# A linear-attention and gated feed-forward block on one core: the second layernorm's sums taken from accumulated outputs, the query exponentials in two pieces, and another order of work

## The chip, the cores and the metric

The kernel runs on one core of a Trainium2 chip. A core has TensorE for matmuls (PE in the profile), VectorE (DVE), ScalarE (ACT), GpSimd (POOL) and SyncE (SP), which here issues DMAs. All of them run their own list of instructions in order and wait for each other by semaphores. SBUF is the working memory, PSUM holds matmul results in eight banks, and HBM the inputs and the output. The metric is the device time of one execution in microseconds; the time before is the median of three runs.

## What is computed

Two residual blocks on `x` of 2048 x 640 in bf16. With `LN(x) = (x - mean) / sqrt(var + 1e-5)`:

```python
qkv = LN(x) @ wqkv                       # 32 heads of 20
pq, pk = q @ w_phi, k @ w_phi            # per head
phi_q = concat([softmax(pq), softmax(-pq)])
phi_k = concat([softmax(pk), softmax(-pk)])
kv, z = phi_k.T @ v, sum(phi_k)          # over the 2048 rows
o = (phi_q @ kv) / (phi_q @ z + 1e-6)
h = x + o @ wo
n = LN(h)
out = h + ((n @ w_gate) * (n @ w_up)) @ w_down   # 640 -> 1536 -> 640
```

## The kernel before

The 2048 rows are 16 tiles of 128 rows (partitions); the 640 columns are five chunks of 128 for the contractions. Names carry the tile's number: `h3` is the residual step of tile 3.

*Prologue.* TensorE runs ten matmuls on zeros (`warm`). The key weights arrive in five row chunks (`wk0` to `wk4`), are transposed on TensorE (`WT`, L392), copied out of PSUM (`WTe`) and folded with `w_phi` (`w5`, masked by `Ph`) into a key-feature weight (`F1`, L411, copied out by `Fe1`). The first tiles of `x` are normalised (`L1s`, `L1a` on VectorE, L428 to L431; `L1l` and `L1e`, a Ln and an Exp, on ScalarE; `L1n` on POOL; `xn`) and transposed on TensorE (`xt`, `xte`). Later tiles are transposed by DMA from SP (`xt4` to `xt15`). The query weights come in by transposing DMAs (`wqt`) and are folded later (`F0`).

*Keys and values.* For each tile, projections `V` and `K` (L482, ten matmuls each), `Ve` copies V out, `Kx` makes the two exponentials, `Ks` sums them (VectorE), `Kr` and `Ke` turn the sums into factors (ScalarE), `Kn` scales (POOL, L518), and `KV` (L526) accumulates over all tiles in two PSUM banks. `KVe` copies the result.

*Queries.* `Q` (L482) fills a pair of PSUM banks; `Qx` makes exponentials with both signs out of it (L553 twice and L554 once for each sign, as a pair's second bank also holds the last 40 columns); `Qs` sums (L557), `Qr`, `Qb`, `Qe`, `Qn` scale one half; `qT` transposes by DMA; `N` (L589) multiplies with the key-value matrix; `dd`, `rd`, `o` (L600, L603, L606) divide; `oT` transposes by DMA (L610); `O` (L616) is the output projection.

*Second layernorm.* `h` (L620) adds the projection to `x` in place. `L2s` takes the statistics of its two halves (L626, L627), `L2a` joins them to mean and variance (L629). `hc` (L638 on VectorE or L639 on ScalarE) writes the centred rows, negated, `hT` transposes them by DMA (L643). The scaling is left until the end, as gate and up are both linear in it: `L2v` adds epsilon on POOL (L630) and `L2r` takes the reciprocal (L632), which `y` applies.

*Feed-forward.* Five blocks of rows (tiles 0 to 1, 2 to 5, 6 to 9, 10 to 13, 14 to 15). Each has 12 pairs of a gate and an up matmul group (`U`, L658, named block, column, 0 or 1); `g` copies the gate out (ScalarE, L663), `u` multiplies it with the up half (VectorE, L666). `D` (L677) is the down projection of a tile, `y` (L689) scales by `L2r`'s result and adds `h`, `w` writes to HBM.

*What sets the order.* The table `PLAN` in the text gives each named operation a place in time, a choice of engine where it has alternatives (`alts`), and its slots (PSUM banks, buffers). `arrange` sorts each engine's operations by that place, and `emit` puts in the semaphore waits that data and slots call for. So the order is written out by hand, engine by engine, and a slot is free once the last user of its previous holder is done. Loads are issued by SP and by ScalarE's queue.

The lines that follow are those that the change touches.

Of the kernel before, what the change touches and what calls it, by code (L numbers as in the profile page):

```python
# [48 lines left out]
x0:0.7:1 w5:1.18:1 wk0:1.18 wv0:4.06 wk1:2.14 wv1:2.62 wk2:1.66:1 wv2:3.58:1 wk3:2.62:1 wv3:4.06 wk4:3.1 wv4:4.54:1 x1:0.7 x2:2.14:1 x3:1.66 x4:3.58:1  # L49
x6:3.1 x8:5.02:1 x10:5.02 x12:4.54:1 x14:21.015 wqt0:13.874 wqt1:9.289 wqt2:26.055 wqt3:6.94 wqt4:19.655 wo0:27.415 wo2:34.715 wd0:35.195 wd1:47.175  # L50
wd2:49.392 wd3:37.595 wg0:32.875 wu0:5.5 wg1:37.115 wu1:6.46 wg2:40.335 wu2:25.575 wg3:36.635 wu3:5.98 wg4:35.675 wu4:36.155 id0:0.9 gl0:1.2 eps:0.7
id1:1.45 gla0:2.07 glb0:2.51 gla4:2.29 glb4:4.51 gla1:2.73 glb1:3.17 gla2:3.39 glb2:4.73 gla3:1.85 glb3:2.95 va1:6.664 phz:3.61 ekz:6.364 rqz:6.064
Sz:7.734 mk0:6.164 mk1:7.484 mk2:7.934 zero:0.7 warm0:1.08 warm1:1.51 warm2:1.94 warm3:2.37 warm4:2.8 warm5:3.23 warm6:3.66 warm7:4.09 warm8:4.52::0
warm9:4.74 Ph0:4.95 Ph1:5.609 Ph2:5.743:1 WT0:4.96::1 WTe0:5.509 WT1:6.769::5 WTe1:7.329:1 WT2:5.836::0 WTe2:6.386 WT3:7.725::2 WTe3:8.85 WT4:8.886::0
WTe4:9.922 F1_0:6.342::6 Fe1_0:8.676:1 F1_1:8.162::4 Fe1_1:9.299 F1_2:7.219::0 Fe1_2:8.052:1 F1_3:9.509::6 Fe1_3:10.766 F1_4:10.953::0 Fe1_4:11.538:1
L1s0:3.993 L1a0:5.633 L1s1:4.813 L1a1:6.1 L1s2:7.03 L1a2:9.686 L1s3:6.21 L1a3:10.215 L1s4:11.145 L1a4:12.785 L1s5:11.965 L1a5:13.005 L1s6:13.115
L1a6:14.353 L1s7:10.325 L1a7:12.895 L1s8:20.053 L1a8:21.803 L1s9:20.983 L1a9:23.833 L1s10:14.463 L1a10:20.873 L1s11:15.283 L1a11:19.443 L1s12:28.423
L1a12:34.233 L1s13:25.363 L1a13:30.243 L1s14:26.183 L1a14:34.123 L1s15:31.773 L1a15:34.013 L1l0:6.132 L1e0:7.229 L1l1:7.009 L1e1:7.952 L1l2:10.546
L1e2:11.389 L1n2:11.899 L1n3:11.699 L1l4:14.835 L1e4:15.678 L1n4:16.588 L1n5:16.188 L1n6:16.388 L1n7:15.988 L1l8:24.376 L1e8:24.806 L1n8:28.209
L1n9:28.409 L1n10:25.45 L1n11:25.65 L1l12:34.675 L1e12:35.518 L1n12:35.895 L1n13:36.095 L1n14:38.854 L1n15:36.295 xn0:7.85::0 xt0:8.53::3 xte0:9.268:1  # L60
xn1:8.35::1 xt1:9.165::1 xte1:9.796:1 xn2:12.875:1:3 xt2:17.252::7 xte2:17.978 xn3:12.161:1:2 xt3:13.17::0 xte3:13.935:1 xn4:19.553::2 xt4:21.495
xn5:17.025:1:0 xt5:18.295 xn6:18.943::1 xt6:22.855 xn7:23.333::3 xt7:24.215 xn8:29.243::1 xt8:30.155 xn9:29.743::3 xt9:31.515 xn10:26.408:1:0
xt10:27.895 xn11:27.745:1:2 xt11:33.355 xn12:36.631:1:0 xt12:45.815 xn13:36.758::1 xt13:38.075 xn14:39.692::2 xt14:47.712 xn15:38.118:1:3 xt15:40.815
V0_0:14.536::0 V0_1:14.807 V0_2:15.079 V0_3:15.351 V0_4:15.622 Ve0:20.238::2 K0_0:9.866::2 K0_1:10.138 K0_2:10.681 K0_3:12.083 K0_4:12.898
# [8 lines left out]
Ks8:41.966::1 Kr8:43.566 Ke8:44.634 Kn8:45.961 KV8:48.538 V9:44.463::4 Ve9:46.092::0 K9:36.997::6 Kx9_0:38.831::2 Kx9_1:39.665 Ks9:40.498::0
Kr9:42.379 Ke9:43.242 Kn9:43.602 KV9:51.842 V10:49.125::6 Ve10:51.708:1:3 K10:46.093::2 Kx10_0:48.562::3 Kx10_1:49.455 Ks10:50.288::3 Kr10:51.925
Ke10:52.788 Kn10:53.419 KV10:56.233 V11:54.874::2 Ve11:57.303:1:1 K11:40.029::4 Kx11_0:41.756::4 Kx11_1:42.619 Ks11:43.452::2 Kr11:45.647 Ke11:49.305
Kn11:50.82 KV11:59.265 V12:63.655::2 Ve12:65.321:1:4 K12:56.548::4 Kx12_0:58.176::0 Kx12_1:59.01 Ks12:59.843::1 Kr12:61.48 Ke12:62.583 Kn12:63.355
# [841 lines left out]
```

## Time and profile before

| | |
|---|---|
| median of 3 runs | 274.31 us (273.6 to 274.59) |
| profiled execution, its span | 272.2 us |
| TensorE busy, instructions | 266.0 us, 2103 |
| VectorE | 171.0 us, 315 |
| ScalarE | 116.6 us, 307 |
| POOL | 73.9 us, 107 |
| `h` (L620) | 16 of 813 ns |
| L626, L627 (statistics of h) | 16 of 481, 16 of 476 ns |
| L629 (aggregate) | 16 of 196 ns |
| L639, L638 (`hc`) | 13 of 828, 3 of 514 ns |
| L553, L554 (`Qx`) | 64 of 442, 32 of 239 ns |
| L518 (`Kn`), L571 (`Qn`), L564 (`Qb`) | 16 each of 2357, 1307, 240 ns |

The profiled execution is one run; its span goes from the first to the last instruction and is 2.1 us under the median. Busy times are unions over an engine's instructions. TensorE's matmuls are pipelined and their ends are modelled, so a stretch shown as fully busy can hold small waits; differences of starts show them.

### The profile page before, as it was taken

How to read it: one execution, taken by the hardware profiler on the slowest of the kernel's cores; microseconds unless marked ns; L12 is line 12 of the kernel's file. 1: busy time of each engine (PE TensorE's matmuls, PEld its weight loads, DVE VectorE, ACT ScalarE, POOL GpSimd, SP SyncE). 2: the span in 40 equal slices, each digit the busy share in tenths (PEclk: the TensorE clock that was granted, in tenths of full speed). 3: DMA queues.
4: the chain of work that ended last, by engine and by line, in shares of the span. 5: the costliest groups of instructions: out<-in, count | busy, mean ns of one | idle time of the engine just before them, and what ended most of it. 6: DMA issues, size and time to landing. Idle time of an engine off the chain costs nothing.

```text
span 272.2 us, 5234 instructions
## 1 busy us (share of the span) xinstructions
PE 266.0 (98%) x2103; PEld 177.2 (65%) x2103; DVE 171.0 (63%) x315; ACT 116.6 (43%) x307; POOL 73.9 (27%) x107
## 2 busy tenths in 40 slices
PE   7899999999989999999999999999999999999996
...
GB/s 201 375 265 162 176 264 313 234 157 108 107 78 160 147 185 110 165 130 98 0 48 48 2 1 43 100 95 43 31 0 2 0 0 51 48 0 0 26 48 55
...
## 3 DMA queue, kind: packets, MB, share of 16 engines
...
q14 instruction: 8, 0.07, 0.1%
HBM read 11.00 MB, written 2.62 MB: 50 GB/s over the span
## 4 chain that ended last, share of the span: by engine, by line
PE 93%; ACT 3%; DMA 2%; ACTq 1%; issue 0%; DVE 0%; DVEq 0%
PE ps L658 38%; PE ps L482 23%; PE ps L677 19%; PE ps L616 8%; DMA ev<-in_A_wqkv_dram 2%; PE ps L526 2%; ACT ph L553 2%; PE ps L589 1%; PE ps L411 1%; ACTq L285 1%; PE ps L462 0%; ACT ph L554 0%; PE ps L392 0%; ACT L884 0%; DVE Wp L689 0%
## 5 line engine op out<-in xcount | busy, mean ns | idle before, releaser
L658 PE MATMUL ps<-xnT,Wgu 128*128 128x512 bf16 (+1 forms) x600 | 105.2, 336 | 0.0
L658 PEld LDWEIGHTS ps<-xnT,Wgu 128*128 128x128 bf16 x600 | 58.5, 98 | 44.2 <-DVE ev L666 0.4
L663 ACT ACTIVATE gt<-ps 128x512 bf16<-128x512 f32 (+1 forms) x60 | 30.5, 511 | 91.4 <-PE ps L658 74.0
L482 PE MATMUL ps<-Wp,xnT 128*128 128x320 bf16 (+1 forms) x480 | 68.6, 299 | 0.8 <-ACT ph L554 0.8
L666 DVE TENSOR_TENSOR ev<-ps,gt 128x512 bf16<-128x512 f32 (+1 forms) x60 | 32.8, 577 | 47.4 <-PE ps L658 34.0
L482 PEld LDWEIGHTS ps<-Wp,xnT 128*128 128x128 bf16 x480 | 45.6, 97 | 18.4 <-ACT ph L554 0.9
L677 PE MATMUL ps<-Wd,ev 128*128 128x320 bf16 (+2 forms) x396 | 53.7, 295 | 0.0
L677 PEld LDWEIGHTS ps<-Wd,ev 128*128 128x128 bf16 x396 | 38.0, 98 | 14.5
L518 POOL TENSOR_TENSOR ek<-ek,SR 128x1280 bf16<-128x1280 bf16 x16 | 37.6, 2357 | 6.7 <-ACT SR L503 6.6
L689 DVE SCALAR_TENSOR_TENSOR Wp<-ps,rs,x_all 128x640 bf16<-128x640 f32 (+3 forms) x18 | 14.5, 808 | 32.9 <-PE ps L677 32.7
L553 ACT ACTIVATE ph<-ps 128x300 bf16<-128x300 f32 x64 | 23.8, 442 | 7.9 <-PE ps L482 7.4
L630 POOL TENSOR_SCALAR ln<-mv 128x1 f32<-128x1 f32 x16 | 3.3, 210 | 84.6 <-DVE mv L629 73.4
L557 DVE TENSOR_REDUCE S<-ph 128x66 f32<-128x1320 bf16 x16 | 24.2, 1515 | 3.1 <-ACT ph L554 3.1
L498 DVE TENSOR_REDUCE SR<-ek 128x64 f32<-128x1280 bf16 x16 | 23.4, 1472 | 1.3 <-ACT ek L494 1.2
L616 PE MATMUL ps<-Wo,Wp 128*128 128x320 bf16 x160 | 23.9, 299 | 0.3 <-ACT RQ L567 0.3
L494 ACT ACTIVATE ek<-ps 128x640 bf16<-128x640 f32 x32 | 22.3, 714 | 2.7 <-PE ps L482 2.4
L571 POOL TENSOR_TENSOR ph<-ph,RQ 128x660 bf16<-128x660 bf16 x16 | 20.9, 1307 | 6.2 <-ACT RQ L567 6.2
L639 ACT ACTIVATE xn<-x_all,mv 128x640 bf16<-128x640 bf16 x13 | 10.7, 828 | 24.2 <-DVE mv L629 24.2
L616 PEld LDWEIGHTS ps<-Wo,Wp 128*128 128x128 bf16 x160 | 15.2, 98 | 6.6 <-issue 0.6
L620 DVE TENSOR_TENSOR x_all<-ps,x_all 128x640 bf16<-128x640 f32 x16 | 13.0, 813 | 4.5 <-PE ps L616 4.4
L606 DVE TENSOR_TENSOR o<-ps,sm 128x720 bf16<-128x720 f32 x16 | 14.2, 894 | 0.1
L428 DVE BATCH_NORM_STATS2 st<-x_all 128x6 f32<-128x320 bf16 x16 | 7.6, 472 | 3.3 <-DMA x_all<-in_A_x_dram 3.3
...
## 6 DMA issues: line engine op xcount, KB each, us to landing
...
```

The source lines that it names most:

```text
L482: ins = e.matmul(pb(b, hb)[:, 0:n1 - n0], lhsT=T["xnT"][:, NC - 1 - c, P * t:P * (t + 1)], rhs=T["Wp"][:, POS[kind], c, n0:n1], start=(c = ...
L494: G.op("act", "%sx%d_%d" % (nm, t, s), lambda e, s=s, b=b, ek=ek: e.activation(out=T["ek"][:, ek.slots[0], 0:2 * D].rearrange("p (b h s f) ...
L498: G.op("dve", "%ss%d" % (nm, t), lambda e, ek=ek, sr=sr: e.tensor_reduce(out=T["SR"][:, sr.slots[0], 0, :], in_=T["ek"][:, ek.slots[0], 0: ...
L518: G.op("pool", "Kn%d" % t, lambda e, ek=ek, sr=sr: e.tensor_tensor(out=T["ek"][:, ek.slots[0], 0:2 * D].rearrange("p (h f) -> p h f", f=DH ...
L553: e.activation(out=o_, in_=i_.rearrange("p (g j f) -> p g j f", j=3, f=DH), func=AF.Exp, scale=1.0 - 2.0 * sg)
L557: G.op("dve", "Qs%d" % t, lambda e, t=t, ph=ph: e.tensor_reduce(out=T["S"][:, t, 0:66].rearrange("p (g k) -> p g k", k=6), in_=pv(ph).rear ...
L571: return e.tensor_tensor(out=v, in0=v, in1=T["RQ"][:, rq.slots[0], 1, 0:33].rearrange("p (g j) -> p g j", j=3).unsqueeze(3).to_broadcast([ ...
L616: ins = e.matmul(pb(b, hb)[:, 0:320], lhsT=T["oT"][:, oT.slots[0], c, :], rhs=T["Wo"][:, c, 320 * hb:320 * (hb + 1)], start=(c == 0), stop ...
L658: ins = e.matmul(pb(b)[:, 0:n], lhsT=T["Wgu"][:, gu, c, P * ft:P * (ft + 1)], rhs=T["xnT"][:, NC - 1 - c, o0:o0 + n], start=(c == 0), stop ...
L663: G.op("act", "g%d_%d" % (bi, ft), lambda e, pg=pg, gt=gt, n=n: e.activation(out=T["gt"][:, gt.slots[0], 0:n], in_=pb(pg)[:, 0:n], func=AF ...
L666: o_ = G.op("dve", "u%d_%d" % (bi, ft), lambda e, pu=pu, gt=gt, hh=hh, ft=ft, n=n: e.tensor_tensor(out=T["hh"][:, hh.slots[0], ft, 0:n], i ...
L677: ins = e.matmul(pb(b, hb)[:, 0:w], lhsT=T["hh"][:, hh.slots[0], ft, P * tt:P * (tt + 1)], rhs=T["Wd"][:, ft, c0 + w * hb:c0 + w * (hb + 1 ...
```

## The change

1. `h` becomes a scalar-tensor-tensor operation (projection times 1.0 plus x) that also writes the row sums. `L2s` and `L2a` fall away. `hc` now computes `sum - 640 h` from that sum, on either engine. A new ScalarE operation `L2q` takes the Square of the same expression and accumulates it over the row; its 640 values per row go to `junk`, ten buffers that lie over `ek`, so that it waits for the last `KV`. `L2v` divides by 640 and adds the epsilon, scaled by 640 squared, and the reciprocal makes up for the factor.
2. `Qx` has two instructions for each sign instead of three: one over 2 x 300 columns of both banks, and the 40.
3. `L1n`, `Kn`, `Qb`, `Qn` and `L2v` may now run on VectorE.
4. All of `PLAN` is replaced: places, engines and slots.

```diff
+H_C = 0.84
...
-                G.op("pool", "L1n%d" % t, lambda e, t=t: e.tensor_scalar(
+                G.op("pool", "L1n%d" % t, lambda e, eng, t=t: e.tensor_scalar(
                     out=T["nb"][:, t:t + 1], in0=T["mv"][:, t, 0:1], scalar1=T["rs"][:, t:t + 1], scalar2=-1.0, op0=ALU.mult,
-                    op1=ALU.mult), 0.2, LP, [rs_b[t], mv_b[t]], [nb_b[t]], 10 * t - 25)
+                    op1=ALU.mult), 0.2, LP, [rs_b[t], mv_b[t]], [nb_b[t]], 10 * t - 25, alts=[("dve", 0.07, LD)])
     KVB = [Buf("kvps%d" % k, "psum") for k in range(2)]
     for t in range(NT):
...
-        G.op("pool", "Kn%d" % t, lambda e, ek=ek, sr=sr: e.tensor_tensor(
+        G.op("pool", "Kn%d" % t, lambda e, eng, ek=ek, sr=sr: e.tensor_tensor(
             out=T["ek"][:, ek.slots[0], 0:2 * D].rearrange("p (h f) -> p h f", f=DH),
             in0=T["ek"][:, ek.slots[0], 0:2 * D].rearrange("p (h f) -> p h f", f=DH),
             in1=T["SR"][:, sr.slots[0], 1, :].unsqueeze(2).to_broadcast([P, 2 * H, DH]), op=ALU.mult),
-            pool_c(1280), LP, [ek, sr], [ek], kk)
+            pool_c(1280), LP, [ek, sr], [ek], kk, alts=[("dve", dve_c(1280), LD)])
         def kv(e, t=t, ek=ek, va=va):
...
-                i0, i1 = pb(b, 0)[:, 0:300], pb(b, 1)[:, 0:300]
-                for o_, i_ in ((v[:, 0:5], i0), (v[:, 5:10], i1)):
-                    e.activation(out=o_, in_=i_.rearrange("p (g j f) -> p g j f", j=3, f=DH), func=AF.Exp, scale=1.0 - 2.0 * sg)
+                e.activation(out=v[:, 0:10].rearrange("p (b g) j f -> p b g j f", b=2),
+                             in_=pp(b, 0, 300).rearrange("p b (g j f) -> p b g j f", j=3, f=DH), func=AF.Exp, scale=1.0 - 2.0 * sg)
...
-            G.op("act", "Qx%d_%d" % (t, sg), qx, 2 * act_c(300) + act_c(40), LA, [b], [ph], kk)
+            G.op("act", "Qx%d_%d" % (t, sg), qx, act_c(600) + act_c(40), LA, [b], [ph], kk)
...
-        def qb(e, rq=rq):
+        def qb(e, eng, rq=rq):
...
-        G.op("pool", "Qb%d" % t, qb, 0.24, LP, [rq], [rq], kk)
+        G.op("pool", "Qb%d" % t, qb, 0.24, LP, [rq], [rq], kk, alts=[("dve", 0.1, LD)])
...
-        G.op("pool", "Qn%d" % t, qn, pool_c(660), LP, [ph, rq], [ph], kk)
+        G.op("pool", "Qn%d" % t, qn, pool_c(660), LP, [ph, rq], [ph], kk, alts=[("dve", dve_c(660), LD)])
...
-        G.op("dve", "h%d" % t, lambda e, t=t, b=b: e.tensor_tensor(
-            out=T["x"][:, t, :].rearrange("p (b n) -> p b n", b=2), in0=pp(b, 0, 320),
-            in1=T["x"][:, t, :].rearrange("p (b n) -> p b n", b=2), op=ALU.add), dve_c(640, True), LD, [b, x_b[t]], [x_b[t]], kk - 2)
-        s2, m2, v2, r2 = Buf("s2%d" % t), Buf("m2%d" % t), Buf("v2%d" % t), Buf("r2%d" % t)
+        sh, sq, v2, r2 = Buf("sh%d" % t), Buf("sq%d" % t), Buf("v2%d" % t), Buf("r2%d" % t)
         rs2_b.append(r2)
-        def l2(e, t=t):
-            e.bn_stats(T["st"][:, t, 0:6], T["x"][:, t, 0:320])
-            return e.bn_stats(T["st"][:, t, 6:12], T["x"][:, t, 320:640])
-        G.op("dve", "L2s%d" % t, l2, 0.82, LD, [x_b[t]], [s2, st_b[t]], kk - 2)
-        G.op("dve", "L2a%d" % t, lambda e, t=t: e.bn_aggr(T["mv2"][:, t, :], T["st"][:, t, :]), 0.11, LD, [s2], [m2], kk - 3)
-        G.op("pool", "L2v%d" % t, lambda e, t=t: e.tensor_scalar(out=T["ln"][:, t:t + 1], in0=T["mv2"][:, t, 1:2], scalar1=EPS_LN,
-                                                               scalar2=None, op0=ALU.add), 0.2, LP, [m2], [v2], kk + 5)
-        G.op("dve", "L2r%d" % t, lambda e, t=t: e.reciprocal(out=T["rs2"][:, t:t + 1], in_=T["ln"][:, t:t + 1]), 0.13, LD, [v2], [r2],
-             kk + 30)
+        G.op("dve", "h%d" % t, lambda e, t=t, b=b: e.scalar_tensor_tensor(
+            out=T["x"][:, t, :].rearrange("p (b n) -> p b n", b=2), in0=pp(b, 0, 320), scalar=1.0,
+            in1=T["x"][:, t, :].rearrange("p (b n) -> p b n", b=2), op0=ALU.mult, op1=ALU.add, accum_out=T["mv2"][:, t, 0:1]),
+            H_C, LD, [b, x_b[t]], [x_b[t], sh], kk - 2)
         hc = Buf("hc%d" % t, "xn")
         def hcf(e, eng, t=t, hc=hc):
             i_ = T["x"][:, t, :].rearrange("p (c n) -> p c n", c=NC)
             if eng == "dve":
-                return e.tensor_scalar(out=rev(hc), in0=i_, scalar1=T["mv2"][:, t, 0:1], scalar2=-1.0, op0=ALU.subtract, op1=ALU.mult)
-            return e.activation(out=rev(hc), in_=i_, func=AF.Identity, scale=-1.0, bias=T["mv2"][:, t, 0:1])
-        G.op("act", "hc%d" % t, hcf, act_c(640, True), LA, [x_b[t], m2], [hc], kk, alts=[("dve", 0.5, LD)])
+                return e.tensor_scalar(out=rev(hc), in0=i_, scalar1=-float(D), scalar2=T["mv2"][:, t, 0:1], op0=ALU.mult, op1=ALU.add)
+            return e.activation(out=rev(hc), in_=i_, func=AF.Identity, scale=-float(D), bias=T["mv2"][:, t, 0:1])
+        G.op("act", "hc%d" % t, hcf, act_c(640, True), LA, [x_b[t], sh], [hc], kk, alts=[("dve", 0.5, LD)])
+        G.op("act", "L2q%d" % t, lambda e, t=t: e.activation(
+            out=T["junk"][:, t % 10, :], in_=T["x"][:, t, :], func=AF.Square, scale=-float(D), bias=T["mv2"][:, t, 0:1],
+            accum_out=T["mv2"][:, t, 1:2]), 0.9, LA, [x_b[t], sh], [sq], kk + 10,
+             after=[kvlast] + ([G.by["L2q%d" % (t - 10)]] if t > 9 else []))
+        G.op("pool", "L2v%d" % t, lambda e, eng, t=t: e.tensor_scalar(
+            out=T["ln"][:, t:t + 1], in0=T["mv2"][:, t, 1:2], scalar1=1.0 / D, scalar2=EPS_LN * D * D, op0=ALU.mult, op1=ALU.add),
+            0.2, LP, [sq], [v2], kk + 15, alts=[("dve", 0.07, LD)])
+        G.op("dve", "L2r%d" % t, lambda e, t=t: e.reciprocal(out=T["rs2"][:, t:t + 1], in_=T["ln"][:, t:t + 1]), 0.13, LD, [v2], [r2],
+             kk + 30)
...
+        T["junk"] = T["ek"].rearrange("p s n -> p (s n)")[:, 0:10 * D].rearrange("p (s n) -> p s n", n=D)
```

The new `PLAN` moves these to another engine. From POOL to VectorE: Kn10, Qn0, Qn2, Qn4, Qb3, Qb10, Qb11, Qb14, L1n5, L1n10 to L1n14, L2v2, L2v3, L2v5, L2v11, L2v12. `hc` runs on VectorE for tiles 0, 4 to 10, 12, 13 and 15 (before: 6, 12, 14). Ve10 to Ve15 run on ScalarE (before: VectorE), WTe0, WTe1, WTe2 and WTe4 on VectorE (before: WTe3). ScalarE's queue issues three loads (x0, x14, wo2; before: ten). The orders at the places that the prediction speaks of:

```
SP, first loads, before:  x1 w5 wk2 wk1 wv1 x6 wv2 wv3 wv4 x10 wu0 wu3 wu1 wqt3 ...
ACT queue, before:        x0 wk0 x3 x2 wk3 wk4 x4 wv0 x12 x8
SP, first loads, after:   w5 x1 wk0 wk2 wk3 wk1 x2 wk4 x3 wv2 x6 wv0 x4 wv1 wv3 x10 wv4 wqt4 wqt0 x8 ...
SP, later, after:         ... xt7 xt6 wqt3 wqt1 wg1 wo0 x12 xt9 xt8 wg2 wd0 wg0 xt11 wd2 wu2 xt10 ...
DVE, first, after:        zero Ph1 L1s0 L1a0 L1s1 xn0 WTe0 L1a1 xte0 xn1 WTe2 WTe1 L1s2 WTe4 ...
TensorE, first, after:    warm x8, WT0, warm x2, xt0 WT2 F1_0 WT3 WT1 xt1 F1_2 WT4 F1_1 F1_3 K0_0 F1_4 ...

TensorE, before:  Q6 KV12 KV13 KV14 KV15 Q7 N1 N3 N0 Q11 Q8 N2 Q14 N9 O1 O0 Q12 N5 O3 Q15 N4 N7 O2 O9 U0 ...
TensorE, after:   KV12 KV13 KV14 KV15 Q6 N1 N3 Q7 N0 Q11 N2 Q14 Q8 O1 N9 Q12 N5 O0 O3 N4 Q15 O2 O9 U0 U0 N7 U0 ...
DVE, after:       KVe0 KVe1 dd1 rd1 o1 dd3 rd3 o3 Qs7 dd0 rd0 o0 Qb10 dd2 rd2 o2 h1 dd9 rd9 o9 dd5 rd5 o5 h0 hc0 ...
SP, after:        oT1 qT13 oT3 oT0 qT7 oT2 oT9 hT1 hT0 qT10 oT4 wd3 oT7 ...
```

PSUM pairs there, before: Q7, Q11, Q14 and O0 follow each other in banks 4 and 5. After: Q11 takes the pair that N1 held, Q14 that of Q7, Q8 that of Q11, and O0 that of O1.

In the first feed-forward block ScalarE now runs, in this order: a gate, `L2q9`, two gates, the two `Qx` of tile 15, and further on `L2q4`, `hc3`, `L2q3` and small Ln and Exp between the gates.

More of the change, by code (lines that the diff above doesn't have):

```diff
@@ L48 @@
 for _t in """
[L49 to L64, printed above, removed]
@@ L73 @@
[L73 to L76, printed above, removed]
@@ L145 @@
-U4_11_1:158.778::2 g4_11:158.502::0 u4_11:161.717 D14_0:251.22::0 y14_0:254.75::1 w14_0:255.681 D15_0:164.918::3 y15_0:167.253::1 w15_0:167.851
-D15_1:267.52::2 y15_1:268.78::2 w15_1:269.245 D15_2:162.89::0 y15_2:164.448::2 w15_2:164.846
+gl0:0.78 gla4:0.942 gla1:1.084 glb1:1.313 gla0:1.452 gla3:1.594 gla2:1.736 glb2:1.965 va1:2.104 eps:2.934 zero:0.91 warm0:1.239 warm1:1.665 warm2:2.091
+warm3:2.517 w5:0.78:1 x0:0.78:1 Ph1:2.585:1 glb4:2.964 ekz:3.103 warm4:2.943 L1s0:3.188 L1a0:4.098 x1:1.26 L1s1:4.207 wk0:1.74:1 L1l0:4.331 L1e0:4.657
@@ new lines @@
+xn0:4.994::0 warm5:3.369 wk2:2.22:1 id0:3.337 id1:3.575 warm6:3.795 warm7:4.221 WT0:4.647::0 glb3:3.82 WTe0:5.506:1 warm8:5.266::1 warm9:5.481 xt0:5.696::1
+WT2:5.974::2 L1a1:5.914 L1l1:6.147 L1e1:6.473 xte0:6.173:1 Ph2:4.048 glb0:4.642 Ph0:4.87 F1_0:6.391::3 Fe1_0:6.909:1 wk3:2.7 WT3:6.71::5 WTe3:7.492:1 wk1:3.18
+WT1:7.128::6 x2:3.66 wk4:4.14:1 x3:4.62:1 xn1:6.711::1 xt1:7.545::7 xte1:8.078 wv2:5.1:1 x6:5.58 WTe2:7.223:1 F1_2:7.824::0 Fe1_2:8.662:1 wv0:6.06:1
+WT4:8.143::3 x4:6.54 WTe1:7.747 F1_1:8.559::4 Fe1_1:9.245 F1_3:8.879::6 Fe1_3:9.829 L1s2:8.155 wv1:7.02 K0_0:9.422::0 WTe4:8.942:1 F1_4:9.694::2 L1s3:9.35
@@ new lines @@
+Kx7_0:32.151::3 V5:31.953::4 Kx7_1:32.736 L1s14:33.089 L1a15:33.876 L1s13:33.985 xt8:28.829 Ve5:33.51::7 wg2:30.139 F0_3:33.309::2 L1a14:34.772 L1n10:34.881:1
+xn10:35.035::3 KV3:33.629 L1s12:35.547 L1a12:36.457 Kr4:34.093 Ke4:34.385 Kn4:34.747 Fe0_3:34.531 Kr6:35.114 V8:33.962::6 Ve8:35.517::0 K9:35.318::4
+F0_0:36.673::2 Kx9_0:36.873::2 Kx9_1:37.458 Ke6:38.041 wd0:30.619 K8:36.992::6 F0_2:38.349::4 L1a13:36.566 Fe0_2:38.865 Fe0_0:37.191:1 L1l12:39.45 L1e12:39.776
+L1n15:40.056 KV4:38.667 Ks7:37.931::3 Kx8_0:39.868::1 wg0:31.099 F0_4:39.001::2 L1n14:40.014:1 Fe0_4:40.059:1 KV5:39.319 xt11:31.579 Kx8_1:40.453 L1n13:40.798:1
@@ L147 @@
+w11_0:262.968 y10_0:262.357::1 w10_0:263.468 D13_0:261.358::2 D15_1:264.618::4 L2r13:263.158 y13_0:264.816::2 y15_1:265.806::0 w13_0:265.728 w15_1:266.251
 """.split():
```

160 lines of the change are left out of this document (82 added, 78 removed).

## The prediction

> **What bounds the kernel now.** I read the page first, then the busy time by stretches, then TensorE in order of time, then the chain that ended last. The page:
>
> ```profile
> span 272.2 us, 5234 instructions
> PE 266.0 (98%) x2103; PEld 177.2 (65%) x2103; DVE 171.0 (63%) x315; ACT 116.6 (43%) x307; POOL 73.9 (27%) x107
> PE 93%; ACT 3%; DMA 2%; ACTq 1%; issue 0%; DVE 0%; DVEq 0%
> ```
>
> TensorE is the engine that ends the kernel. The change adds and removes no matmul (both programs issue the same 2103), so all it can win is time in which TensorE waits, and all it can lose is new waiting. The stretches (columns: window, its busy time, then PE, PEld, DVE, ACT, POOL busy, clock, DMA share, GB/s) say where it waits:
>
> ```profile
> 0.00:10.00 10.00, 7.48 (x55) 3.93 (x56) 5.75 (x15) 4.82 (x11) 5.91 (x29) 1.00 0.84 259
> ...
> 60.00:70.00 10.00, 10.00 (x84) 7.25 (x82) 8.43 (x8) 8.28 (x30) 9.68 (x9) 1.00 0.72 117
> 70.00:80.00 10.00, 9.20 (x128) 7.19 (x126) 9.18 (x14) 6.92 (x31) 8.41 (x10) 1.00 0.38 72
> 80.00:90.00 10.00, 9.70 (x96) 6.93 (x95) 10.00 (x19) 6.23 (x27) 4.74 (x7) 1.00 0.93 175
> ...
> 260.00:273.00 13.00, 9.65 (x76) 7.03 (x74) 3.07 (x4) 0.00 (x0) 0.00 (x0) 1.00 0.16 54
> ```
>
> So: the prologue, the stretch from 76 to 96 us where the query work turns into the feed-forward blocks, and the tail. The middle one in TensorE's order of time (start, time, what, idle before):
>
> ```profile
> 77.38 1.18 PE L589 MATMUL ps<-KVm,scratch 128*128 128x63 bf16 x33
> 79.35 2.91 PE L482 MATMUL ps<-Wp,xnT 128*128 128x300 bf16 x20 [0.80 <-ACT ph L554]
> 82.09 0.50 PE L589 MATMUL ps<-KVm,scratch 128*128 128x63 bf16 x11
> 82.59 1.54 PE L482 MATMUL ps<-Wp,xnT 128*128 128x300 bf16 x10
> 83.97 0.49 PE L589 MATMUL ps<-KVm,scratch 128*128 128x63 bf16 x11
> 84.31 1.52 PE L616 MATMUL ps<-Wo,Wp 128*128 128x320 bf16 x10
> 86.13 1.52 PE L616 MATMUL ps<-Wo,Wp 128*128 128x320 bf16 x10 [0.29 <-ACT RQ L567]
> ```
>
> Starts say more than busy times. From N1 (77.38) to the first U0 (95.74) are 18.36 us. The work there is 5 Q projections, 5 O and 8 N, at the pitch that undisturbed ones have in the chain (1.37, 1.36, 0.33): 6.85 + 6.80 + 2.64 = 16.29. So TensorE loses 2.07 us. Two things make it late. Q11 takes the PSUM pair that Q7 held, and starts at 79.35 when Q7's last exponential (L554) has ended; Q14 waits in the same way for Q11, O0 for Q14. And U0 needs the transposes of tiles 0 and 1: O0 ends at 87.49, `h` starts at 88.75 behind other VectorE work, the statistics (L626, L627, L629) end at 90.87, `hc` runs at 91.22, the transpose is issued at 93.06 and lands at 95.69, 0.05 us before U0. VectorE is busy all of 80 to 90.
>
> [...]
>
> **The change, part by part.**
> *Statistics.* Per tile VectorE loses two BATCH_NORM_STATS2 (481 and 476 ns) and the aggregate (196): 1.15 us, 18.4 in all. `h` becomes a SCALAR_TENSOR_TENSOR with a summed output. The trace has none with a sum; `h` now is 813 ns, the same op in `y` (L689, with a pointer scalar) 884, and the sum's surcharge lies between 0 and the aggregate's 0.20: I take 0.10, 1.6 us in all. ScalarE gains 16 Squares of 128x640 with a pointer bias, as L639 (828 ns), plus 0 to 0.29 (the row of the smallest Ln, 128x1) for the sum: I take 0.95, 15 us. What hides them: in the first feed-forward block, TensorE work of 13.2 (12 pairs) plus 3 us of O and N set between, ScalarE has 12 gates of 0.38, 3 Squares, one query exponential pair (1.6), small Ln and Exp (1.6) and one `hc`: 11.5 of 16. They would decide only at over 2 us each. The result is awaited by `y` alone, behind the D matmuls, over 10 us later.
> By the Trainium skill ("VectorE: DVE Perf Modes", section "Two Vector instructions with no wait between them") an op that writes its accumulator is two instructions; that would put the surcharge at the upper end, 0.20, and U0, which also waits for h2's PSUM pair, 0.1 later. No row here shows it.
> *Exponentials.* Two 300-wide ones (pair 0.73 to 0.74 us) become one of 600. Between 442 (300 wide) and 714 ns (640 wide) a 600 costs 0.68: 0.06 less, twice per tile, 2 us of ScalarE in all, and 0.12 off each release of a Q's PSUM pair. Bounds 0 and 0.12.
> *Moves.* Eight more `hc` on VectorE (11 instead of 3; 514 against 828 ns): +4.1 VectorE, -6.6 ScalarE. Kn10, Qn0, Qn2, Qn4, four Qb, six L1n and five L2v leave POOL for VectorE: by nearest rows 1.5 + 3 x 0.85 + 15 x 0.15 = 6.3. Ve10 to Ve15 go back to ScalarE (6 x 820 against 716 ns). VectorE: 171.0 - 18.4 + 1.6 + 4.1 + 6.3 - 4.9 = about 160; ScalarE: 116.6 + 15 - 2 - 6.6 + 4.3 = 127. Both stay far below 266. No moved item costs by itself; what counts is who is late.
> *Middle.* In the new order Q7 stands behind N1 and N3, Q11 takes the pair of N1 (freed by o1), Q8 that of Q11, so Q projections alternate over three pairs. From N1 to U0 TensorE now has 6 Q, 5 O and 7 N: 8.22 + 6.80 + 2.31 = 17.3 us. Is U0's input there by then? O0 stands after 5 Q, 6 N and O1: 6.85 + 2.0 + 1.36 = 10.2, ends at 11.6 after N1. Ahead of `h0` VectorE has six dd+rd+o (1.25 each), Qs7 (1.4), a Qb and h1: 10 us, so it waits for O0. Then h0 0.9, `hc0` on VectorE 0.5, hops 0.3: 13.3. SP by then has 8 transposes at 1.4 behind o1 (at about 2): 13.2. So hT0 is issued at about 13.4 and lands 2.64 later: 16.0, 1.3 us early. The 2.07 us should go; I take 1.8, since h2's pair (U0 takes it) leaves under 0.4 us of room. Bounds 1.2 and 2.07.
> *Prologue.* From WT0 (5.39) to K0 (10.78) TensorE has 5.39 us for 5 WT, 2 xt, 4 F1: 7 x 0.28 + 4 x 0.32 = 3.2. It waits for the wk loads, which land at 4.44, 6.20, 7.54, 8.62 and 9.85 because SP and ScalarE's queue interleave nine 160 KB units there, 0.60 each. Now SP issues w5, x1, the wk with only x2 between, then the rest: wk4 should land near 8. ScalarE no longer issues loads, so the first Ln is not behind them, and xn0 (8.59 now, behind a Ln that stood behind a copy) can run near 6. Against it: on VectorE the mask product Ph1 stands ahead of the first statistics and needs w5, and four of the five WT evacuations are there instead of one. L1s0 3.9, its chain of 0.9 + 0.2 + 0.3 + 0.2 + 0.55 and hops: xt0 6.5; xn1 ends 8.2; two more evacuations, then two folds: K0 about 10.2. I take -0.6; ends +0.4 (w5 lands at 4.62 as now, and everything behind Ph1 waits) and -1.0.
> *Loads.* The same bytes; SP now carries all but three. xt8 stands behind wg1, wo0 and x12. Tail: D15_1, y15_1, its store, as now: 2.5 us after the last matmul.
> Sum: 272.2 - 0.6 - 1.8 = 269.8 us of span. The median of the runs stands 2.1 above the profiled span (274.31 to 272.2): **271.9 us**. With all bounds: 272.2 - 1.0 - 2.07 - 0.7 (the scattered gaps, of which V8's 0.17 is one) gives 270.5, and 272.2 + 0.4 - 1.2 gives 273.5.
>
> **Rivals.** *The middle stays as it is* (a wait takes the place of the one removed). For it: SP is a chain of 1.4 us transposes there, VectorE was full from 80 to 90, and Q projections still wait for work of other engines to free their pairs. Then only the prologue is won: 273.7. Against it: per tile 1.05 us less between `h` and `hc`. Chance 0.23.
> *Late transposes* (slower). xt8 has 1024 KB of weights and x just ahead instead of 704; at the 0.30 MB/us of the landings from 42.4 to 49.1 (2016 KB in 6.71) that adds 1.07 to its 4.2 us: 5.3. It is issued near 29 by the issues ahead of it, and V8's place on TensorE is 10.2 + 24.6 = 34.8, so there is 0.5 us. But xt13 took 9.94 us in the loaded stretch. If xt8 does, TensorE stops for 4.1 at V8: 271.9 + 4.1 = 276.0. It decides, against the gain, once xt8 takes over 8.2 us. For it: V8 already waits 0.17 for xt8 (landed 35.19, V8 at 35.24). Against: xt8 now stands ahead of wd0, wg0 and wg2. Chance 0.13.
> The forecast has 0.64.
>
> **How the numbers follow.** A measurement of this kernel tells 0.5% (1.4 us) from nothing, so faster is under 272.9. The forecast's own range is 270.5 to 273.5, of its chance 0.02 above 272.9; the second case is within, the third slower. Faster 0.64 - 0.02 = 0.62, same 0.23 + 0.02 = 0.25, slower 0.13. Up to 274.3 the range takes in the second case and leaves out the third.
>
> **What would show it.** Right: K0 before 10.6; Q11, Q14 and O0 without a wait for L554 or its like; U0 17.3 to 17.6 after N1; no BATCH_NORM left after 80 us; `h` at 0.8 to 1.0 us; ScalarE near 127 busy. Wrong: gaps over 0.3 us between TensorE's starts after 30 us, above all at V8, K9 and U0, or gates late behind a Square with TensorE waiting for their PSUM bank.

## The result, and the profile after

| | before | after |
|---|---|---|
| median | 274.06 us (273.6 to 274.59, 4 runs) | 275.94 us (275.52 to 276.19, 4 runs) |
| span of the profiled execution | 272.2 us | 274.1 us |
| ratio, 95% interval | | 1.0068 [1.0049, 1.0088] |

The kernel became slower by 0.7%; the prediction was 271.9 us. First the page of the kernel after (the span, the engines' busy time, and the engines' shares in the chain that ended last):

```profile
span 274.1 us, 5191 instructions
PE 265.9 (97%) x2103; PEld 176.5 (64%) x2103; DVE 173.0 (63%) x310; ACT 121.3 (44%) x299; POOL 67.9 (25%) x88
PE 81%; DVE 13%; ACT 3%; POOL 1%; issue 1%; DVEq 0%; ACTq 0%; POOLq 0%
```

TensorE's work is the same. VectorE lost 18 us of statistics and yet is busier than before (171.0), and it now holds 13% of the chain, where it had 0%. The stretches (window, its busy time, then PE, PEld, DVE, ACT, POOL busy, clock, DMA share, GB/s) say where:

```profile
50.00:60.00 10.00, 10.00 (x84) 7.26 (x82) 10.00 (x8) 9.28 (x26) 6.29 (x8) 1.00 1.06 233
60.00:70.00 10.00, 9.83 (x82) 6.86 (x80) 10.00 (x7) 8.87 (x29) 8.78 (x7) 1.00 0.70 110
70.00:80.00 10.00, 7.32 (x110) 5.51 (x109) 9.34 (x9) 5.88 (x19) 8.57 (x8) 1.00 0.39 74
```

VectorE is full from 50 to 70 us, with 14 instructions in 20 us (one lies over 60 and is counted in both rows), and TensorE loses its time behind that, from 70 to 80. TensorE in order of time there (start, time, what, idle before), just behind the last keys:

```profile
73.41 0.51 PE L520 MATMUL ps<-ev,ek 128*128 128x63 bf16 x11 [0.16 <-ACT ev L245]
74.42 0.51 PE L520 MATMUL ps<-ev,ek 128*128 128x63 bf16 x11 [0.50 <-POOL ek L512]
75.31 0.51 PE L520 MATMUL ps<-ev,ek 128*128 128x63 bf16 x11 [0.39 <-ACT ev L245]
75.67 1.53 PE L476 MATMUL ps<-Wp,xnT 128*128 128x300 bf16 x10
78.83 0.85 PE L582 MATMUL ps<-KVm,scratch 128*128 128x63 bf16 x22 [1.63 <-DVE KVm L527]
```

The last `KV` ends a little earlier than before (75.82, before 76.17). But `N1` waits for `KVe`, the copy of the key-value matrix on VectorE, and starts at 78.83 instead of 77.38. The chain of waits, followed back from there (start, us, engine, tile, line):

```profile
49.82 2.96 DVE S L550 x2
52.78 1.39 DVE SR L492
...
57.00 1.27 DVE RQ L557
58.27 1.50 DVE ek L512
59.77 1.40 DVE SR L492
61.16 1.52 DVE ph L564
62.68 2.87 DVE S L550 x2
65.56 1.39 DVE SR L492
66.95 2.69 DVE ph L564
69.64 1.40 DVE SR L492
71.04 1.43 DVE S L550
72.47 2.60 DVE ph L564
...
77.94 0.84 DVE KVm L527 x2
```

For 29 us (but for 0.75 that the view calls issue) the chain is VectorE alone, one instruction behind the other, up to the copy that `N1` waits for. Among the sums (L550, L492) stand the moved pieces: Qb3 (L557), Kn10 (L512), Qn0, Qn2 and Qn4 (L564). Qb3 and the three Qn are far longer than the prediction priced them (0.15 us a Qb, 0.85 a Qn). Below, VectorE's own rows and POOL's in order of time; each of these four lies over a POOL instruction and ends 0.05 (Qb3) or 0.70 us (each Qn) behind it:

```profile
56.92 1.35 DVE L557 TENSOR_TENSOR RQ<-RQ 128x32 f32<-128x32 f32 x1
58.19 1.57 DVE L512 TENSOR_TENSOR ek<-ek,SR 128x1280 bf16<-128x1280 bf16 x1
61.08 1.60 DVE L564 TENSOR_TENSOR ph<-ph,RQ 128x660 bf16<-128x660 bf16 x1
66.87 2.77 DVE L564 TENSOR_TENSOR ph<-ph,RQ 128x660 bf16<-128x660 bf16 x1
72.39 2.68 DVE L564 TENSOR_TENSOR ph<-ph,RQ 128x660 bf16<-128x660 bf16 x1
```

```profile
55.86 2.36 POOL L512 TENSOR_TENSOR ek<-ek,SR 128x1280 bf16<-128x1280 bf16 x1
58.70 3.28 POOL L512 TENSOR_TENSOR ek<-ek,SR 128x1280 bf16<-128x1280 bf16 x1 [0.28 <-ACT SR L497]
61.95 1.91 POOL L564 TENSOR_TENSOR ph<-ph,RQ 128x660 bf16<-128x660 bf16 x1
66.58 2.36 POOL L512 TENSOR_TENSOR ek<-ek,SR 128x1280 bf16<-128x1280 bf16 x1
69.70 4.67 POOL L512 TENSOR_TENSOR ek<-ek,SR 128x1280 bf16<-128x1280 bf16 x2
```

Qb3 starts 1.06 us into POOL's `Kn` (55.86 to 58.22) and ends at 58.27. Qn2 starts 0.29 us into a later one (66.58 to 68.94) and ends 0.70 after it, at 69.64. The other way round, POOL's `Kn` at 58.70, which meets Kn10 on VectorE, takes 3.28 us instead of 2.36, and its `Qn` at 61.95 takes 1.91 instead of 1.31. The two engines seem to take turns. VectorE's sums, which read one input, are not held: the one at 69.56, beside `Kn` on POOL, takes 1.47 us. That is a reading of overlaps so far; the experiments test it.

### The profile page after: what moved, and what is told of

Read it like the earlier page. It is cut to its first block, busy times and chain, and to the rows that moved or that the text cites. A ratio compares the mean times of both kernels' runs of the same rounds, so it can differ in the third digit from the quotient of the medians.

```text
span 274.1 us, 5191 instructions
## 1 busy us (share of the span) xinstructions
PE 265.9 (97%) x2103; PEld 176.5 (64%) x2103; DVE 173.0 (63%) x310; ACT 121.3 (44%) x299; POOL 67.9 (25%) x88
## 4 chain that ended last, share of the span: by engine, by line
PE 81%; DVE 13%; ACT 3%; POOL 1%; issue 1%; DVEq 0%; ACTq 0%; POOLq 0%
PE ps L652 38%; PE ps L671 19%; PE ps L476 13%; PE ps L609 7%; DVE S L550 5%; DVE SR L492 3%; DVE ph L564 2%; PE ps L582 2%; ACT ph L545 1%; PE ps L520 1%; PE ps L405 1%; DVE RQ L557 1%; DVE o L599 1%; DVE ek L512 1%; ACT Wp L245 0%
## 5 line engine op out<-in xcount | busy, mean ns | idle before, releaser
L652 PE MATMUL ps<-xnT,Wgu 128*128 128x512 bf16 (+1 forms) x600 | 107.5, 336 | 0.0
L657 ACT ACTIVATE gt<-ps 128x512 bf16<-128x512 f32 (+1 forms) x60 | 29.2, 510 | 90.6 <-PE ps L652 65.9
L512 POOL TENSOR_TENSOR ek<-ek,SR 128x1280 bf16<-128x1280 bf16 x15 | 36.1, 2418 | 4.2 <-ACT SR L497 4.2
L545 ACT ACTIVATE ph<-ps 128x600 bf16<-128x600 f32 x32 | 21.2, 676 | 6.5 <-PE ps L582 3.4
L550 DVE TENSOR_REDUCE S<-ph 128x66 f32<-128x1320 bf16 x16 | 23.9, 1512 | 0.3 <-ACT ph L547 0.2
L492 DVE TENSOR_REDUCE SR<-ek 128x64 f32<-128x1280 bf16 x16 | 23.4, 1470 | 0.2 <-ACT ek L488 0.2
L488 ACT ACTIVATE ek<-ps 128x640 bf16<-128x640 f32 x32 | 20.9, 699 | 1.8 <-PE ps L476 1.4
L564 POOL TENSOR_TENSOR ph<-ph,RQ 128x660 bf16<-128x660 bf16 x13 | 17.5, 1355 | 10.5 <-ACT RQ L560 10.3
L626 ACT ACTIVATE ek<-x_all,mv 128x640 bf16<-128x640 bf16 x16 | 13.2, 824 | 10.9 <-DVE x_all L615 10.7
L630 POOL TENSOR_SCALAR ln<-mv 128x1 f32<-128x1 f32 x11 | 2.1, 192 | 58.2 <-ACT ek L626 57.7
L615 DVE SCALAR_TENSOR_TENSOR x_all<-ps,x_all 128x640 bf16<-128x640 f32 x16 | 13.1, 819 | 4.5 <-PE ps L609 4.5
L245 ACT ACTIVATE ev<-ps 128x640 bf16<-128x640 f32 x16 | 11.4, 710 | 0.9 <-PE ps L476 0.4
```

The costliest lines, as they stand in the source:

```text
L488: G.op("act", "%sx%d_%d" % (nm, t, s), lambda e, s=s, b=b, ek=ek: e.activation(out=T["ek"][:, ek.slots[0], 0:2 * D].rearrange("p (b h s f) ...
L492: G.op("dve", "%ss%d" % (nm, t), lambda e, ek=ek, sr=sr: e.tensor_reduce(out=T["SR"][:, sr.slots[0], 0, :], in_=T["ek"][:, ek.slots[0], 0: ...
L512: G.op("pool", "Kn%d" % t, lambda e, eng, ek=ek, sr=sr: e.tensor_tensor(out=T["ek"][:, ek.slots[0], 0:2 * D].rearrange("p (h f) -> p h f", ...
L545: e.activation(out=v[:, 0:10].rearrange("p (b g) j f -> p b g j f", b=2), in_=pp(b, 0, 300).rearrange("p b (g j f) -> p b g j f", j=3, f=D ...
L550: G.op("dve", "Qs%d" % t, lambda e, t=t, ph=ph: e.tensor_reduce(out=T["S"][:, t, 0:66].rearrange("p (g k) -> p g k", k=6), in_=pv(ph).rear ...
L564: return e.tensor_tensor(out=v, in0=v, in1=T["RQ"][:, rq.slots[0], 1, 0:33].rearrange("p (g j) -> p g j", j=3).unsqueeze(3).to_broadcast([ ...
```

## The experiments

Theory L (lock): a VectorE instruction that reads both inputs from SBUF, and a POOL instruction that reads SBUF, run one after the other; Kn10, Qn and Qb on VectorE stand still for that, VectorE becomes the chain, and `KVe` is late. Rival S: these forms are as slow as that on VectorE by themselves. Rival O: the new order loses on its own, whichever engine scales. The numbers E1 to E13 are those of the labels; there is no E8. Ratios are to the kernel before, run on the same chip.

**E1 and E7: POOL writes, and reads nothing.** E1 replaces POOL's 15 `Kn` by one fill with a constant, E7 by two; both leave out the scaling of the key features there.

```diff
+            if eng == "pool":
+                e.memset(pad_t, 0.05)        # E7 only
+                return e.memset(ek_t, 0.05)
             return e.tensor_tensor(out=ek_t, in0=ek_t, in1=factors, op=ALU.mult)
```

> The changed kernel, with the same order on every engine, but POOL's 15 scalings of the key features (Kn) are replaced by a fill of the same 128x1280 with a constant: POOL then writes there and reads nothing, and the key features' scaling is left out. Theory L (lock): in the changed kernel a VectorE operation with two SBUF inputs (Qn, Qb, Kn10) waits while POOL runs one that reads SBUF, and the wait is what made Qn 2348 ns and Qb 793 ns on VectorE. Then Qn0, Qn2, Qn4 fall to 0.7 to 0.9 us each, Qb3 to 0.2, TensorE's N1 comes before 76.5 us (78.83 now), and the time is 270 to 272.5. Rival S (slow form): this form with a broadcast operand is simply slow on VectorE. Then Qn stays at 2.2 to 2.4 and the time at 274 or more, helped only by POOL's shorter fills.

> As E1, but each Kn on POOL becomes two fills (one of them into unused columns), so that POOL is busy as long as with Kn (2.33 us) and still reads nothing. Lock: Qn0, Qn2, Qn4 stay at 0.84 us, Qb3 under 0.25, N1 at 75.5 to 77, 272.0 to 273.4 us. Rival (E1 won because POOL was done sooner, not because VectorE went free): Qn on VectorE is short, but N1 is at 78 or later and the time 275 us or more.

E1: 272.02 us, 0.9912 [0.9893, 0.9932]. E7: 272.16 us, 0.991 [0.9876, 0.9945]. The moved pieces on VectorE, by form, after:

```profile
L564 DVE TENSOR_TENSOR ph<-ph,RQ 128x660 bf16<-128x660 bf16 x3 | 7.0, 2348 | 0.0
L557 DVE TENSOR_TENSOR RQ<-RQ 128x32 f32<-128x32 f32 x4 | 3.2, 793 | 0.3 <-ACT RQ L553 0.3
```

and in E7, with POOL's fills:

```profile
L567 DVE TENSOR_TENSOR ph<-ph,RQ 128x660 bf16<-128x660 bf16 x3 | 2.5, 836 | 0.0
L560 DVE TENSOR_TENSOR RQ<-RQ 128x32 f32<-128x32 f32 x4 | 2.0, 500 | 0.3 <-ACT RQ L556 0.3
```

```profile
L515 POOL MEMSET ev<- 128x1280 bf16 x15 | 17.5, 1164 | 4.3 <-ACT SR L497 4.2
L516 POOL MEMSET ek<- 128x1280 bf16 x15 | 17.5, 1164 | 0.0
```

The same three `Qn` take 836 ns instead of 2348, so rival S falls. Qb3 takes 184 ns instead of 1350, while Qb10 (929) and Qb14 (694), which still meet a `Qn` on POOL, stay as in after (931, 701); that is why the mean is 500. Kn10 came first and was hardly held: 1484 ns in E7, 1575 in after. In E1 one could still say that POOL was simply done sooner, as one fill is half as long as `Kn`. In E7 POOL is busy for 2.33 us per tile as with `Kn`, and nothing changes against E1: N1 at 75.22 (E1 75.52), first U at 93.25, VectorE 2% of the chain. What cost the time is the meeting of the two engines' reads, not POOL's time. VectorE's sums take 1.48 us beside these fills, as beside `Kn`: with one SBUF input they are not held. Rival O falls too: without the lock the new order is 0.9% faster than the kernel before.

In the Trainium skill, "SBUF — State Buffer", section "Who interferes with whom", this is a rule: a VectorE instruction with two SBUF inputs contends with a GpSimd instruction that reads SBUF, and not with one that only writes, and the second to come stands until the first is through. The trace agrees on both halves: 2348 ns beside `Kn`, 836 beside a fill. This is the rule that speaks against the change, and the prediction does not weigh it.

**E2 and E3: all eight scalings back on POOL.** E2 changes the engine alone; E3 also puts Qn2, Qn4 and their transposes behind Kn14, and two mask steps early.

```diff
+for _n in ("Kn10", "Qn0", "Qn2", "Qn4", "Qb3", "Qb10", "Qb11", "Qb14"):
+    PLAN[_n] = (PLAN[_n][0], 0, PLAN[_n][2])
+# E3 only: Qn2 at 71.6, Qn4 at 71.65, qT2 at 72.6, qT4 at 72.7, mk1 and mk2 at 53.23
```

> The changed kernel with Kn10, Qn0, Qn2, Qn4 and four Qb back on POOL, at the same places in time. Theory L: VectorE loses 11.8 us of busy time (173.0 to about 161), POOL gains 7.3 and loses the 0.9 that its own Kn waited; POOL becomes the chain between 52 and 76 us, Kn14 ends near 76.4 (74.37 now), N1 at 77.5 to 78.5, time 274.0 to 275.6. Rival W (the new order and the accumulated sums are slow by themselves, whoever runs the eight): 275.9 plus or minus 0.4, with VectorE still the chain before N1.

> As the run before, and Qn2 and Qn4 (with their transposes) stand behind Kn14 on POOL, and the mask's two selects earlier. Theory L: POOL reaches the end of Kn14 at about 74 by the sum of its rows, VectorE is no longer late, N1 at 75.5 to 76.5, time 271.8 to 273.5, faster than both kernels. Rival W: 275.9 as before.

Both missed. E2: 277.23 us, 1.01 [1.0078, 1.0122]. E3: 276.31 us, 1.0074 [1.0049, 1.01]. VectorE is free (162.6 us busy in E2), but now POOL is the chain. In E2, TensorE, the stretch from 70 to 80 us, and POOL:

```profile
77.42 1.32 PE L522 MATMUL ps<-ev,ek 128*128 128x63 bf16 x22 [2.73 <-POOL ek L514]
78.56 2.43 PE L478 MATMUL ps<-Wp,xnT 128*128 128x300 bf16 x10
```

```profile
70.00:80.00 10.00, 7.06 (x85) 5.11 (x84) 5.41 (x5) 5.03 (x16) 9.59 (x10) 0.85 0.48 89
```

```profile
53.09 0.24 POOL L559 TENSOR_TENSOR RQ<-RQ 128x32 f32<-128x32 f32 x1 [2.52 <-ACT RQ L555]
```

The new order gave POOL 2.52 us of nothing at 50.6, as its next items had gone to VectorE and ScalarE's factors for the rest come later; with the items back, Kn14 ends at 77.36 (after: 74.37). The wait costs TensorE a second time: behind it the granted clock is down, to a mean of 0.85 from 70 to 80 us, where the kernel after has 1.00. By starts, the two last `KV` and Q6 take 3.41 us up to N1, and the same work takes 2.06 in E3 with the clock at 1.00. E2's miss is 1.63 us over the range, so most of it may be this clock (1.35). A wait of about 2 us does not always do it: the clock fell behind one of 1.95 us (E9's trace) and not behind one of 2.00 (E3's).

In E3 Kn14 is early enough, and the late Qn2 and Qn4 take its place in POOL's row: Qb5 and Qb13 come behind them. ScalarE and TensorE in E3:

```profile
78.08 0.23 ACT L564 ACTIVATE RQ<-RQ 128x32 f32<-128x32 f32 x1 [2.55 <-POOL RQ L561]
79.92 0.23 ACT L564 ACTIVATE RQ<-RQ 128x32 f32<-128x32 f32 x1 [1.47 <-POOL RQ L561]
81.39 0.21 ACT L551 ACTIVATE ph<-ps 128x40 bf16<-128x40 f32 x1
```

```profile
81.66 0.51 PE L586 MATMUL ps<-KVm,scratch 128*128 128x63 bf16 x11 [2.00 <-ACT ph L551]
```

ScalarE waits for POOL twice, with Qe5 and Qe13, and Qx6 stands behind both in its order. N0 takes the PSUM pair of Q6, so it waits until Qx6 is through at 81.60: TensorE stops for 2.17 us by the pitch of its starts. So the move to VectorE answered a real need: with everything back on it, POOL is late in this order, before the last key or just behind it.

**E4, E5, E6: the exponentials and the sums, each in the order of before.** E4 takes over part 2 alone, E5 part 1 alone (each `L2q` right behind its `hc`, five of them between 100 and 109 us), E6 both.

```diff
 # E4, E6: Qx as in part 2 of the change;  E5, E6: h, hc, L2q, L2v as in part 1
+    _s = {1: 100.3, 0: 101.95, 2: 103.3, 9: 104.3, 3: 108.5}.get(_t, PLAN["hc%d" % _t][0] + 0.01)
+    PLAN["L2q%d" % _t] = (_s, 0, ())
```

> The kernel before, with the query exponentials in two pieces alone (its own order). By the 0.06 us for each sign (676 instead of a pair of 735 ns) a Q's PSUM pair comes free 0.12 us earlier, and two to four such releases stand on the chain from 76 to 87 us: 0.2 to 0.5 us faster, 273.6 to 273.9. Rival: nothing that can be measured (274.06), as VectorE and SP end the chain there.

> The kernel before with part 1 alone (sums from h's accumulator and from Squares on ScalarE), its order kept. Theory: of the 2.07 us lost between N1 and U0 the part that hangs on h0 to hc0 goes, as VectorE loses 1.05 us for each tile there: hc0 starts near 90.0 instead of 91.22, U0 at 94.7 to 95.3 instead of 95.74, 273.0 to 273.7 us. Rival (SP's row of transposes decides, not VectorE): hc0 is earlier, U0 stays at 95.7, 274.0 to 274.6. Rival (the Squares delay the gates): gaps at TensorE after 100 us, over 275.

> The kernel before with parts 1 and 2, its order kept. Theory: as with part 1 alone, 0.0 to 0.3 less, 272.8 to 273.6 us, as the shorter exponentials did nothing by themselves. Rival (they pay once h is short): 272.5 or less, U0 before 94.5.

E4: 274.78 us, 1.0007 [0.9986, 1.0029]. E5: 275.24, 1.0025 [1.0006, 1.0044]. E6: 274.98, 1.0024 [1.0002, 1.0045]. None wins. In E5 `h0` ends 0.76 us sooner after N1 than before (11.42 against 12.18), but `hc0` starts at the same distance (13.83 against 13.84). The reason is neither VectorE nor SP. ScalarE's order in E5:

```profile
91.15 0.74 ACT L560 ACTIVATE ph<-ps 128x300 bf16<-128x300 f32 x2
91.75 0.23 ACT L561 ACTIVATE ph<-ps 128x40 bf16<-128x40 f32 x1
91.83 0.86 ACT L638 ACTIVATE xn<-x_all,mv 128x640 bf16<-128x640 bf16 x1
```

`hc0` (L638) stands behind the second exponential of a query tile and starts when that ends, in E5 as before. So the statistics were hidden there, and removing them alone buys nothing. The small loss is a wait of 0.64 us at 113.57, before a `D`, where the kernel before had none. It hangs on a Square: VectorE stands for 0.91 us at `L2r`, until 112.84, as `L2v` on POOL comes behind the Square and a Qn, and the `u` that this `D` needs stands behind it.

**E9 to E13: can the order do without VectorE?** All have the eight scalings on POOL and leave nothing out, and each removes the wait that the one before showed. E9 fills POOL's hole at 50.6; E10 adds Kn13 ahead of Qb2 and Qn4 behind Kn14; E12 adds Qb2 ahead of Kn13 and mk1, mk2 early; E13 adds Qe13 behind Qx6. E11 is E10 with the old sums.

```diff
+# E9:  Ke11 48.9, Kn11 50.0, Qr3 48.17, Qb3 49.9, Qe3 50.95, Qn3 52.2, qT3 54.3
+# E10: Kn13 62.3, Qn4 72.1, qT4 73.2
+# E12: Qb2 62.2, mk1 53.234, mk2 53.235
+# E13: Qe13 75.31, Qn13 75.4
```

> The changed kernel with all eight scalings back on POOL, and POOL's idle time from 50.6 to 54 us filled as it was before: Ke11, Kn11, Qr3, Qb3, Qe3, Qn3 and qT3 earlier. Theory (the rest of the new order is sound; what lost was VectorE locked by POOL, and in the second and third experiment a POOL that started 2 to 3 us late): POOL's last Kn14 ends at 72 to 73.5, N1 at 75.5 to 76.5, 271.5 to 273.3 us. Rival (the order loses by itself, whatever engine scales): N1 at 78 or later, 275 us or more.

> As E9, with two places changed on POOL: Kn13, whose factors were ready 3.6 us before it ran, goes ahead of Qb2 and Qn9, which made POOL wait 0.97 us, and Qn4 with its transpose goes behind Kn14. Nothing is left out. Theory (POOL's row of scalings up to Kn14 is what E9 still lost): Kn14 ends at 73.0 to 73.6 instead of 75.28, TensorE's gap of 2.10 us before KV14 shrinks under 0.5, N1 at 76.3 to 77.0, 272.1 to 273.2 us, near the two kernels whose POOL read nothing. Rival (as in the third experiment, a late Qn takes the place: qT4's landing or a held ph buffer stops TensorE by N4 or a Q): the gap moves behind 80 us, 274 us or more.

> As E10, with three small places changed on POOL: Qb2 ahead of Kn13 (in E10 ScalarE stood 1.62 us at Qe2, behind it Kx14, Kr12 and Ke12, until Qb2 had come after Kn13), and the mask steps mk1 and mk2 early, where POOL waits anyway, so that Qn4 comes 0.6 us sooner behind Kn14. Nothing is left out. Theory (the late Qn4 held the ph buffer for Qx7, and with it TensorE for 1.04 us at N0): measured from the first K, Kn14 ends 0.3 to 0.6 us and Qn4 0.9 to 1.2 us sooner than in E10 (63.82 and 65.73), the gap at N0 falls under 0.4, 272.4 to 273.3 us, ratio to the kernel before under 0.996. Rival (the row of POOL cannot be shortened by places): the gap stays at N0 or moves, 273.6 to 274.5.

> As E12, with Qe13 behind Qx6 in ScalarE's order. In E12 TensorE still lost 0.92 us at N0, for a reason other than the ph buffer: Qx6, whose input and buffer were ready at 75.8, stood behind Qe13, which waited until 76.82 for POOL's Qb13; Qx7 and with it N0's PSUM pair came after. Theory: Qx6 starts about 1.2 us sooner, the gap at N0 falls under 0.2, and 0.5 to 0.9 us of it reach the end: 272.0 to 272.5 us at a kernel before of 274.3, ratio 0.988 to 0.993. Rival (the next wait stands close behind, Q11's pair or N2): the gap moves by a few us and the ratio stays over 0.993.

| | median us | ratio | Kn14's end after the first K | TensorE's largest wait by its starts, 50 to 100 us |
|---|---|---|---|---|
| after (VectorE locked) | 275.94 | 1.0068 [1.0049, 1.0088] | 64.34 | 1.79 before N1 |
| E9 | 274.59 | 1.0008 [0.9982, 1.0035] | 65.15 | 2.10 before KV14 |
| E10 | 273.91 | 0.9997 [0.9978, 1.0015] | 63.82 | 1.04 before N0 |
| E12 | 272.89 | 0.9942 [0.992, 0.9964] | 63.28 | 0.92 before N0 |
| E13 | 272.71 | 0.9929 [0.9908, 0.995] | 64.11 | 0.73 before an O at 92.13 |

E9 and E10 won less than expected, E12 as much. E9's wait was POOL's row, as the theory said, but longer, and in its trace the clock fell behind it as in E2 (0.83 from 70 to 80 us). In E10 the rival came in, a late query tile, though not by the held buffer that was given as the reason: ScalarE stood 1.47 us at Qe13, as in E3, with Qx6 and so N0 behind it, and Qx7, which takes the buffer, followed Qx6 without a wait. E12 brought Qn4 1.19 us nearer to the first K, the time fell as forecast, and the wait at N0 stayed:

```profile
78.56 0.51 PE L588 MATMUL ps<-KVm,scratch 128*128 128x63 bf16 x11 [0.76 <-ACT ph L553]
```

ScalarE stood there at Qe13 again, for 1.47 us. E13 took that wait away, and another of 0.73 us came up 14 us later, so E13 is not told apart from E12 (its 64.11 holds 0.6 us that TensorE lost in this profile at an early transpose, at 15.38). Both are faster than either kernel given.

> As E10, with part 1 undone: the old adding h, the statistics of h (two and an aggregate) behind it on VectorE, no Squares. VectorE has 1.05 us more for each tile between h and hc. Theory (in the new order h0 to hT0 stands just ahead of the first U, so here the sums pay): hc0 starts 1.0 to 2.2 us later than in E10, the first U 0.5 to 2 us later behind its N1, 0.5 to 2 us over E10. Rival (SP's row of transposes or the PSUM pairs decide, as with the sums put alone into the kernel before): U not later, within 0.4 us of E10 or under it.

E11: 282.28 us, 1.0298 [1.0277, 1.0318], 8.4 us over E10. The expected size was 0.5 to 2. From 90 to 110 us (the windows of E11):

```profile
90.00:100.00 10.00, 7.40 (x61) 4.92 (x59) 9.65 (x19) 2.33 (x6) 0.24 (x1) 1.00 0.46 89
100.00:110.00 10.00, 8.56 (x79) 6.80 (x80) 9.62 (x20) 4.40 (x16) 3.28 (x6) 1.00 0.52 100
```

VectorE is nearly full and TensorE waits for it: 2.3 us in two waits for `h` (in this kernel L625), whose PSUM pair the next U takes, and 0.6 for an `o`. Two more waits for an `o`, of 1.3 and 1.0 us, stand at 142.56 and 149.25. In the new order, where most `hc` are on VectorE just ahead of the first feed-forward block, the sums are worth 8.4 us; in the order of before, nothing. E11 keeps the places that were made for the short version, so a part of the 8.4 may be its own order.

## Why the prediction was wrong

*Moves* is the step that failed: "No moved item costs by itself; what counts is who is late." It priced Qn on VectorE at 0.85 us and a Qb at 0.15, and added VectorE's load up to 160 us, far below TensorE. The price alone was right (836 and 184 ns where POOL reads nothing), but not beside POOL: Qn 2348, Qb 793 on the mean. E7 with the same order and engines takes VectorE from 173.0 to 167.7 us busy and the time from 275.94 to 272.16. So the forecast of 271.9 is nearly what the change gives without the lock, and nearly all of the miss (3.78 of 4.04 us) is that one resource. N1 is 3.61 us later in after than in E7; 1.81 of that is there already at the last `KV` (75.82 against 74.01), the rest is `KVe`. A second, smaller fault of the same sum: five more `xn` went from ScalarE to VectorE (14 instead of 9, 599 ns each, 3.0 us), which the list of moves leaves out, and were not counted; E7 has them too and loses nothing by them. They are 3.0 of the 7.7 us by which E7's VectorE is over the 160; the rest was not traced. ScalarE, without them, is at 121.3, not 127.

*The bound by busy time.* "Both stay far below 266" compared totals of the whole span, while VectorE before already had 8.43 of 10 us from 60 to 70. Qn0 and Qn2 fall into that stretch of after. In E7, where they take 836 ns each, the stretch is busy for 8.64 us; at 1600 and 2768 ns it is full (10.00).

*Middle.* Nearly right: Q11, Q14 and O0 start without a wait, and N1 to the first U take 18.03 us in E7, of which 17.3 was forecast as work and 0.59 is a wait behind Qb10, locked as well (0.85 us in the chain there). That is over the 17.6 named as the upper end. In after it is 18.43. The first U comes at 93.25 in E7, 2.49 us sooner than before (95.74), but 0.33 of that is N7, which now stands behind it; 0.6 + 1.8 was forecast. The reason given for the delay before was partly wrong: E5 shows that `hc0` waited for ScalarE, not for the statistics. What helped was probably the new place of `hc` on VectorE and the sums together (E5 and E11 have one without the other, and both lose); no run takes them apart further.

*Statistics.* Both surcharges were near: `h` 819 ns and the read of its sum 82 more (forecast 0.10 over 0.81), the Square 824 and 193 (forecast 0.95):

```profile
L615 DVE SCALAR_TENSOR_TENSOR x_all<-ps,x_all 128x640 bf16<-128x640 f32 x16 | 13.1, 819 | 4.5 <-PE ps L609 4.5
L615 DVE DVE_READ_ACCUMULATOR x_all<-ps,x_all 128x1 f32 x16 | 1.3, 82 | 0.0
L626 ACT ACTIVATE ek<-x_all,mv 128x640 bf16<-128x640 bf16 x16 | 13.2, 824 | 10.9 <-DVE x_all L615 10.7
L626 ACT ACTIVATION_READ_ACCUMULATOR ek<-x_all,mv 128x1 f32 x16 | 3.1, 193 | 0.0
```

The rule cited there, of two instructions for one with an accumulator, holds, and ScalarE shows the same; but the second one costs VectorE 82 ns, not the 0.20 us of the upper end.

*Exponentials.* 676 ns for 600 columns (forecast 680), and alone worth nothing (E4).

*Prologue.* K0 started at 10.03 (forecast 10.2, before 10.78). This moves by itself: the same prologue gave 9.81 in E11 and 11.64 in E10, where TensorE waited 0.98 us for the load of a weight chunk.

*Late transposes.* Did not happen: xt8 took 3.71 us, V8 started at 34.65 without a wait. That this rival's 276.0 lies next to the measured 275.94 is chance.

*What would show it.* The test named as wrong, "gaps over 0.3 us between TensorE's starts after 30 us", is what the trace shows, but the places named for it (V8, K9, U0) were not the ones.
